# Linear attention in pairs of chunks: one score product, one output copy and one subtraction for two chunks of 128 tokens

## Chip, cores and metric

The program runs on one core of a Trainium2 chip. The metric is the device time of one execution in microseconds (us); lower is better. Engine names are those of the profile: PE is TensorE, PEld its weight loads, DVE is VectorE, ACT is ScalarE, POOL is GpSimd, SP is SyncE, which here only issues transfers.

## What is computed

Three layers follow one another. The first, which the change touches, is linear attention with a decay per head; then a gated feed-forward layer with a convolution over three tokens, then a mixture of eight experts.

```python
for t in range(S):                      # B, H, S, D = 2, 8, 768, 64
    state = gamma * state + einsum('bhd,bhe->bhde', k[:, :, t], v[:, :, t])
    y[:, :, t] = scale * einsum('bhd,bhde->bhe', q[:, :, t], state)
x = y in token order                    # (2, 768, 512)
h = relu(x @ w_in); gate = sigmoid(conv3(h)); x = (h * gate) @ w_out
out = prob[e] * (relu(x @ w1[e]) @ w2[e])   # e chosen per token
```

## The kernel before

All of the program is issued in an order written out by hand; each engine works through its own list in that order and waits on semaphores.

**Attention.** Two heads are handled together, one on the lower and one on the upper 64 partitions, so there are 8 head pairs ("heads" below). A head is cut into 6 chunks of 128 tokens, 48 chunks in all. For a chunk, `scores(c)` makes one 128 x 256 product of the keys with the two heads' queries (tile `s_ps`, L279) and multiplies it on DVE by the decays (tile `at`, L281). `output(c)` makes the chunk's addition to the state (tile `inc`, L287), which DVE adds into the state in two instructions, one per head (`st`, L292 and L294); then two products of the padded values `vz` with `at`, and one of the state before the chunk with the decayed queries, into `y` (L297 and L299). ACT copies `y` out as the upper part of a split number (L301), and DVE subtracts that copy to get the lower part (L302). That subtraction is returned as a function and is issued one chunk later. All these products are in 32-bit floats, and each shows as two records per product in the trace.

**The loop** (L424 to L447) issues `scores` of chunk i, then `output` of chunk i - 2, then the subtraction of the chunk before, then `advance()`. `advance()` moves the side work on by a step: `prepare()` of the next head (copies of the queries on ACT, the decay of queries on POOL at L253, the decay of keys on ACT, and the padded values at L274), and `convert()` for the 16 pieces of the weights `w_in` and `w_out`, which arrive as 64-bit words. A conversion fetches a piece into `raw` (L143), runs two instructions on DVE (L149, L150) and one on ACT (L151), one on POOL (L153) and the split into two parts (L171, L173). The table `STARTS` says at which chunk a conversion begins, its DVE part coming six steps later, and `LOADS` says at which chunk the loads of a head's keys, queries and values are issued. From chunk 25 on, products of the feed-forward layer (tile `h_ps`, L133 to L135) fill in between, at a rate of 0.7 slices of three products a chunk.

**Buffers.** `vz` holds the padded values of a whole head, and there is one of it. `at` has 3 buffers, `inc` one, `s_ps` and `y` two each, and each head of a lane of two has two state tiles.

Of the kernel before, what the change touches and what calls it, by code (L numbers as in the profile page):

```python
# [23 lines left out]
P = 128  # L24
# [67 lines left out]
def tile_kernel(ctx, tc, cat, cst, qT, kT, kN, vN, w_in, conv_w, w_out, wg, w1, w2, out):  # L92
# [105 lines left out]
    vz = p1.tile([P, NCH, 2, P], F32, name="vz")  # L198
    zst = [p1.tile([P, P], F32, name=f"st{i}") for i in range(4)]
# [14 lines left out]
    po.memset(vz[:, :, 0, 64:128], 0.0)  # L214
    po.memset(vz[:, :, 1, 0:64], 0.0)
    xT = {}

    class Head:


        def __init__(self, b, hp, lane):
            self.b, self.hp = b, hp
            self.g = [1.0 - 2.0 ** (-5.0 - (2 * hp + j)) for j in range(2)]
            self.qz, self.st, self.at = qz[lane], zst[2 * lane:2 * lane + 2], {}
# [15 lines left out]
        def prepare(self):  # L240
            hp = self.hp
            qd = ca[:, hp, C_QD:C_QD + CH]
            for c in self.parts:
# [10 lines left out]
                for j in range(2):  # L254
# [6 lines left out]
                    if len(self.parts) > 1:  # L261
                        self.values(c, j)
                    yield 1

            if len(self.parts) == 1:
                yield 1
                for c in (range(3), range(3, 6)):
                    for j in range(2):
                        self.values(c, j)
                    yield 3  # L270

        def values(self, c, j):
            p = slice(64 * j, 64 * j + 64)
            se.activation(out=vz[:, c.start:c.stop, j, p], in_=self.kv[:, 1, c.start:c.stop, p], func=AF.Copy)  # L274

        def scores(self, c):
            tok = slice(c * CH, (c + 1) * CH)
            ps = ps1.tile([P, 2, CH], F32, tag="s", name="s_ps")
            te.matmul(ps, self.kq[:, 0, tok], self.qz[:, :, tok], start=True, stop=True)  # L279
            self.at[c] = p1.tile([P, 2, CH], F32, tag="at", name="at", bufs=3)  # L280
            ve.tensor_tensor(out=self.at[c], in0=ps, in1=self.dm, op=ALU.mult)  # L281

        def output(self, c):
            at = self.at.pop(c)
            if c + 1 < NCH:
                inc = ps1.tile([P, P], F32, tag="i", name="inc", bufs=1)
                te.matmul(inc, self.kv[:, 0, c, :], self.kv[:, 1, c, :], start=True, stop=True)  # L287
                old, new = self.st[c % 2], self.st[(c + 1) % 2]
                for j in range(2):
                    pj = slice(64 * j, 64 * j + 64)  # L290
                    if c == 0:
                        ve.tensor_copy(out=new[pj, pj], in_=inc[pj, pj])  # L292
                    else:
                        ve.scalar_tensor_tensor(out=new[pj, pj], in0=old[pj, pj], scalar=self.g[j] ** CH, in1=inc[pj, pj], op0=ALU.mult, op1=ALU.add)  # L294
            y = ps1.tile([P, CH], F32, tag="y", name="y")
            for j in range(2):
                te.matmul(y, vz[:, c, j, :], at[:, j, :], start=(j == 0), stop=(c == 0 and j == 1))  # L297
            if c > 0:
                te.matmul(y, self.st[c % 2], self.q1[:, c, :], start=False, stop=True)  # L299
            hi, lo = (self.x[:, i, c * CH:(c + 1) * CH] for i in range(2))  # L300
            se.activation(out=hi, in_=y, func=AF.Copy)  # L301
            return lambda: ve.tensor_tensor(out=lo, in0=y, in1=hi.bitcast(F32), op=ALU.subtract)  # L302
# [92 lines left out]
    seq = [(p, c) for p in range(8) for c in range(NCH)]  # L395
# [21 lines left out]
    rest = None  # L417
    LOOK = 2
# [4 lines left out]
    slices = 0  # L423
    for i in range(len(seq) + LOOK):  # L424
        if i < len(seq):
            p, c = seq[i]
            heads[p].scores(c)
            if i == 0:
# [3 lines left out]
            if i in STARTS:  # L432
                running.append([convert(*parts.pop(0)), 1])
            if i in LOADS:
                load(LOADS[i])
# [621 lines left out]
```

## Time and profile before

| | |
|---|---|
| time, median of 3 runs | 437.85 us (436.75 to 440.81) |
| profiled execution | 436.14 us |
| its span, first to last instruction | 434.4 us |
| around the span | 1.74 us |
| mean granted TensorE clock | 0.991 of full speed |

The profiled execution lies 1.71 us under the median. Attention takes the first 90 us of the span; the feed-forward layer and the routing follow, and from about 260 us the experts. In the timelines a row that stands for several instructions of one kind gives the first start and the time to the last end. Busy times of PE include the drain of a product through the array, so that two products that follow at once overlap in the view; the distance between two starts is the cost of one.

### The profile page before, as it was taken

The page shows a single profiled execution, that of the slowest core. Times are in us where ns is not written, and L with a number is a line of the kernel's source. Part 1 is how long each engine was busy: PE and PEld are TensorE (multiplying, and loading weights), DVE is VectorE, ACT ScalarE, POOL GpSimd, SP SyncE. Part 2 cuts the span into 40 slices and gives each one's busy share as a digit, 9 for nine tenths or more (in the row PEclk, how much of TensorE's full clock was granted, in tenths as well). Part 3 has the DMA queues.
Part 4 walks back from the last instruction along what each step waited for, and adds up shares of the span by engine and source line. Part 5 has one row for each costly group of instructions (what it writes and reads, how often), then busy time and mean ns, then how long its engine had stood idle before and what let it go on. Part 6 is the DMA issues. An engine that isn't in the chain of part 4 may idle for free.

```text
span 434.4 us, 7297 instructions
## 1 busy us (share of the span) xinstructions
PE 411.6 (95%) x2412; PEld 327.6 (75%) x2412; DVE 290.0 (67%) x518; ACT 259.9 (60%) x429; POOL 91.1 (21%) x92
## 2 busy tenths in 40 slices
PE   8988999997999999999899999999999999999992
PEld 7877997896998778988678776666757667777781
DVE  3798789788766350477789157757775875867750
ACT  2787776676666212576614167756776866767660
POOL 4256664213000000000000330124033213101210
PEclk9999999998999999999999999999999999999998
DMA  7989673320000101000197898999999998984001
GB/s 238 382 298 392 245 234 86 88 83 0 2 0 2 48 28 47 25 0 2 29 382 246 318 354 286 353 395 409 386 366 313 382 364 285 352 308 150 22 27 48
DMA packets 27324, 86.59 MB, mean 199 GB/s; under 512 B 3598, under 2 KB 4622, under 8 KB 27280
## 3 DMA queue, kind: packets, MB, share of 16 engines
q1 hardware_dynamic: 25200, 79.76, 50.8%
q0 software_dynamic: 2080, 6.29, 3.8%
q8 instruction: 21, 0.34, 0.3%
q14 instruction: 23, 0.19, 0.1%
HBM read 105.18 MB, written 6.55 MB: 257 GB/s over the span
## 4 chain that ended last, share of the span: by engine, by line
PE 30%; issue 26%; DMA 18%; DVE 17%; ACT 6%; POOL 1%; SPq 1%; POOLq 0%; DVEq 0%; ACTq 0%
DMA out_dram<-yo,it 16%; DVE cc L350 4%; PE x_ps L133 4%; PE x_ps L134 3%; PE x_ps L135 3%; PE h_ps L133 3%; PE y L297 3%; PE h_ps L134 3%; PE h_ps L135 3%; PE s_ps L279 2%; DVE cc L354 2%; DVE na L149 2%; ACT cc L347 2%; PE inc L287 1%; DMA kq<-in_qT_dram 1%
## 5 line engine op out<-in xcount | busy, mean ns | idle before, releaser
L133 PE MATMUL h_ps<-xT,wih 128*128 128x384 f32 x128 | 47.1, 368 | 2.3 <-ACT wc L192 2.3
L350 DVE SCALAR_TENSOR_TENSOR cc<-h,cw,cc 128x768 f32<-128x768 f32 x32 | 35.0, 1095 | 18.0 <-ACT cc L347 18.0
L859 POOL DMA_INDIRECT out_dram<-yo,it x13 | 17.7, 1359 | 137.7 <-ACT yo L858 137.7
L723 POOL DMA_INDIRECT xg<-xs,it x13 | 17.3, 1332 | 126.8 <-DMA qc<-in_w_dram 118.9
L134 PE MATMUL h_ps<-xT,wih 128*128 128x384 f32 x128 | 43.8, 342 | 0.0
L135 PE MATMUL h_ps<-xT,wil 128*128 128x384 f32 x128 | 43.7, 341 | 0.0
L133 PE MATMUL x_ps<-woh,hg 128*128 128x512 f32 x96 | 38.6, 402 | 0.0
L134 PE MATMUL x_ps<-wol,hg 128*128 128x512 f32 x96 | 37.5, 391 | 0.0
L135 PE MATMUL x_ps<-woh,hg 128*128 128x512 f32 x96 | 37.4, 390 | 0.0
L714 DVE TENSOR_TENSOR wc<-r,wc 128x1024 fp32r<-128x1024 f32 x22 | 26.0, 1221 | 15.4 <-ACT wc L713 15.4
L714 DVE TENSOR_TENSOR ws0l<-r,ws0l 128x1024 fp32r<-128x1024 f32 x22 | 26.0, 1222 | 11.2 <-ACT ws0l L713 11.0
L714 DVE TENSOR_TENSOR ws1h<-r,ws1h 128x1024 fp32r<-128x1024 f32 x22 | 26.0, 1222 | 10.5 <-ACT ws1h L713 10.0
L297 PE MATMUL y<-at,vz 128*128 128x128 f32 x192 | 30.6, 281 | 1.2 <-DVE xT L302 0.6
L714 DVE TENSOR_TENSOR ws0h<-r,ws0h 128x1024 fp32r<-128x1024 f32 x22 | 26.0, 1222 | 7.7 <-ACT ws0h L713 7.6
L279 PE MATMUL s_ps<-qz,kq 128*128 128x256 f32 x96 | 29.1, 385 | 1.0 <-issue 1.0
L153 POOL TENSOR_TENSOR na<-na,raw 128x512 int32<-128x512 int32 (+1 forms) x17 | 21.9, 1288 | 38.2 <-DVE na L150 12.6
L713 ACT ACTIVATE ws0l<-r 128x1024 fp32r<-128x1024 f32 x22 | 22.1, 1052 | 13.1 <-PE y L135 13.1
L713 ACT ACTIVATE wc<-r 128x1024 fp32r<-128x1024 f32 x22 | 22.1, 1055 | 11.9 <-PE g L135 11.9
L133 PEld LDWEIGHTS h_ps<-xT,wih 128*128 128x128 f32 x128 | 24.6, 192 | 5.5 <-ACT wc L192 2.6
L297 PEld LDWEIGHTS y<-at,vz 128*128 128x128 f32 x192 | 25.3, 191 | 3.8 <-DVE xT L302 2.3
L281 DVE TENSOR_TENSOR at<-s_ps,ca 128x256 f32<-128x256 f32 x48 | 20.2, 421 | 11.8 <-PE s_ps L279 11.7
L713 ACT ACTIVATE ws1h<-r 128x1024 fp32r<-128x1024 f32 x22 | 22.1, 1053 | 6.5 <-PE g L135 6.2
(231 smaller groups left out, 1027.3 us busy)
## 6 DMA issues: line engine op xcount, KB each, us to landing
r<-in_w_dram SPq DMA_DIRECT2D x88, 512.0 KB
qc<-in_w_dram SPq DMA_DIRECT2D x32, 512.0 KB
qs1l<-in_w_dram SPq DMA_DIRECT2D x32, 512.0 KB
raw<-in_w_in_dram SPq DMA_DIRECT2D x8, 512.0 KB
raw<-in_w_out_dram SPq DMA_DIRECT2D x8, 512.0 KB
kq<-in_qT_dram SPq DMA_DIRECT2D x7, 384.0 KB
kq<-in_kT_dram SPq DMA_DIRECT2D x7, 384.0 KB
kv<-in_vN_dram SPq DMA_DIRECT2D x7, 384.0 KB
```

The lines of the kernel that those rows point to most:

```text
L133: te.matmul(ps, lhi, rhi, start=first, stop=False)
L134: te.matmul(ps, lhi, rlo, start=False, stop=False)
L135: te.matmul(ps, llo, rhi, start=False, stop=last)
L153: po.tensor_tensor(out=a, in0=a, in1=lo, op=ALU.add)
L279: te.matmul(ps, self.kq[:, 0, tok], self.qz[:, :, tok], start=True, stop=True)
L281: ve.tensor_tensor(out=self.at[c], in0=ps, in1=self.dm, op=ALU.mult)
L297: te.matmul(y, vz[:, c, j, :], at[:, j, :], start=(j == 0), stop=(c == 0 and j == 1))
L350: ve.scalar_tensor_tensor(out=cc, in0=h[:, i:i + S], scalar=cw[:, m, i:i + 1], in1=cc, op0=ALU.mult, op1=ALU.add)
L713: se.activation(out=w[:, 0, h, :], in_=r, func=AF.Copy)
L714: ve.tensor_tensor(out=w[:, 1, h, :], in0=r, in1=w[:, 0, h, :].bitcast(F32), op=ALU.subtract)
L723: return po.indirect_dma_start(out=xg, out_offset=None, in_=xs[0:n], in_offset=bass.IndirectOffsetOnAxis(ap=it[:, j:j + 1], axis=0), bound ...
L859: po.indirect_dma_start(out=out, out_offset=bass.IndirectOffsetOnAxis(ap=it[:, j:j + 1], axis=0), in_=yo, in_offset=None, bounds_check=NT ...
```

## The change

Attention goes on by pairs of chunks. `scores(c, u)` makes two products into the two halves of one bank of `s_ps` and one multiplication of 128 x 512 by the decays, which are repeated by a broadcast. The padded values are made there as well: two copies on ACT for the two chunks of the pair, in one of two small tiles `vz`; `prepare()` makes none any more. `output(c)` makes both additions to the state in one bank of `inc`, four state updates in a row (two for a head's last pair), and the four products of `at` with the values. The products with the state are made later, in `rest()`, after a slice of the feed-forward layer and a step of the side work; there is one copy of 128 x 256 by ACT, and one subtraction of 128 x 256, issued a pair later. Each lane has three state tiles, and `at` two buffers. The loop runs over 24 pairs and looks one pair ahead, not two chunks.

```diff
-    vz = p1.tile([P, NCH, 2, P], F32, name="vz")
-    zst = [p1.tile([P, P], F32, name=f"st{i}") for i in range(4)]
+    vz = [p1.tile([P, 2, 2, P], F32, name=f"vz{i}") for i in range(2)]
+    zst = [p1.tile([P, P], F32, name=f"st{i}") for i in range(6)]
...
-        def scores(self, c):
-            tok = slice(c * CH, (c + 1) * CH)
-            ps = ps1.tile([P, 2, CH], F32, tag="s", name="s_ps")
-            te.matmul(ps, self.kq[:, 0, tok], self.qz[:, :, tok], start=True, stop=True)
-            self.at[c] = p1.tile([P, 2, CH], F32, tag="at", name="at", bufs=3)
-            ve.tensor_tensor(out=self.at[c], in0=ps, in1=self.dm, op=ALU.mult)
+        def scores(self, c, u):
+            ps = ps1.tile([P, 2, 2, CH], F32, tag="s", name="s_ps")
+            for i in range(2):
+                tok = slice((c + i) * CH, (c + i + 1) * CH)
+                te.matmul(ps[:, i], self.kq[:, 0, tok], self.qz[:, :, tok], start=True, stop=True)
+            for j in range(2):
+                pj = slice(64 * j, 64 * j + 64)
+                se.activation(out=vz[u][:, :, j, pj], in_=self.kv[:, 1, c:c + 2, pj], func=AF.Copy)
+            at = p1.tile([P, 2, 2, CH], F32, tag="at", name="at", bufs=2)
+            ve.tensor_tensor(out=at, in0=ps, in1=self.dm.unsqueeze(1).to_broadcast([P, 2, 2, CH]), op=ALU.mult)
...
+            n = 2 if c + 2 < NCH else 1
+            for i in range(n):
+                te.matmul(inc[:, i, :], self.kv[:, 0, c + i, :], self.kv[:, 1, c + i, :], start=True, stop=True)
...
+            y = ps1.tile([P, 2, CH], F32, tag="y", name="y", bufs=2)
+            for i in range(2):
+                for j in range(2):
+                    te.matmul(y[:, i, :], v[:, i, j, :], at[:, i, j, :], start=(i == 0 and j == 0), stop=False, skip_group_check=True)
+
+            def rest():
+                for i in range(2):
+                    if c + i > 0:
+                        te.matmul(y[:, i, :], self.st[(c + i) % 3], self.q1[:, c + i, :], start=False, stop=True, skip_group_check=True)
+                hi, lo = (self.x[:, i, c * CH:(c + 2) * CH].rearrange("p (c t) -> p c t", t=CH) for i in range(2))
+                se.activation(out=hi, in_=y, func=AF.Copy)
+                return lambda: ve.tensor_tensor(out=lo, in0=y, in1=hi.bitcast(F32), op=ALU.subtract)
...
+            heads[p].scores(c, n % 2)
...
+            for i in (2 * n, 2 * n + 1):
+                if i in STARTS:
+                    running.append([convert(*parts.pop(0)), 1])
+                if i in LOADS:
+                    load(LOADS[i])
...
+        if n:
+            p, c = seq[n - 1]
             rest = heads[p].output(c)
-        if todo:
-            todo()
+        if low:
+            low()
+        fill(2 * n)
         advance()
+        if n:
+            low = rest()
+        fill(2 * n + 1)
+        advance()
```

**Where instructions move.** On SP, which issues the transfers, the start of the program: `cs`, `wgs` and `in_conv_w_dram` are small constants, `kq` and `kv` are the loads of the third head, and `raw` is the first piece of `w_in`. Before:

```order
L410 DMA cs<-in_cst_dram 128x531
L411 DMA wgs<-in_wg_dram 128x36
L143 DMA raw<-in_conv_w_dram 128x48
L143 DMA raw<-in_w_in_dram 128x1024
L230 DMA kq<-in_qT_dram 128x768
L231 DMA kq<-in_kT_dram 128x768
L233 DMA ca<-in_cat_dram 128x386
L234 DMA kv<-in_vN_dram 128x768
L235 DMA kv<-in_kN_dram 128x768
```

The same place now:

```order
L412 DMA cs<-in_cst_dram 128x531
L413 DMA wgs<-in_wg_dram 128x36
L143 DMA raw<-in_conv_w_dram 128x48
L231 DMA kq<-in_qT_dram 128x768
L232 DMA kq<-in_kT_dram 128x768
L234 DMA ca<-in_cat_dram 128x386
L235 DMA kv<-in_vN_dram 128x768
L236 DMA kv<-in_kN_dram 128x768
L143 DMA raw<-in_w_in_dram 128x1024 x3
```

The load of the third head belongs to chunk 1, which is now issued together with chunk 0 and ahead of the first step of the side work, so the first piece of `w_in` has moved behind its five transfers.

On DVE, around the first conversion (L149 and L150, which read that piece), before; the first `at` is that of chunk 6 (chunks count from 0 over all heads), the one behind the conversion that of chunk 7:

```order
L281 TENSOR_TENSOR at<-s_ps,ca 128x256
L294 SCALAR_TENSOR_TENSOR st_108<-st_107,inc 64x64 x2
L302 TENSOR_TENSOR xT<-y,xT 128x128
L149 TENSOR_SCALAR na<-raw 128x512
L150 SCALAR_TENSOR_TENSOR na<-raw,na 128x512
L281 TENSOR_TENSOR at<-s_ps,ca 128x256
L302 TENSOR_TENSOR xT<-y,xT 128x128
L281 TENSOR_TENSOR at<-s_ps,ca 128x256
L292 COPY st_110<-inc 64x64 x2
```

And now; the first `at` is that of chunks 6 and 7, the one behind the conversion that of chunks 8 and 9:

```order
L274 TENSOR_TENSOR at<-s_ps,ca 128x512
L290 SCALAR_TENSOR_TENSOR st_110<-st_109,inc 64x64 x2
L302 TENSOR_TENSOR xT<-y,xT 128x256
L149 TENSOR_SCALAR na<-raw 128x512
L150 SCALAR_TENSOR_TENSOR na<-raw,na 128x512
L274 TENSOR_TENSOR at<-s_ps,ca 128x512
L288 COPY st_112<-inc 64x64 x2
L290 SCALAR_TENSOR_TENSOR st_113<-st_112,inc 64x64 x2
L302 TENSOR_TENSOR xT<-y,xT 128x256
```

The conversion stands at the same step of the side work. The state updates behind it (`st_112` is the state after chunk 6) now feed PE within the same pair, as can be seen on PE in the second head's first pair, chunks 6 and 7:

```order
L269 MATMUL s_ps<-qz_105,kq 128x256 x2
L282 MATMUL inc<-kv 128x128 x2
L294 MATMUL y<-at,vz_107 128x128 x4
L299 MATMUL y<-kq,st_112 128x128
L269 MATMUL s_ps<-qz_105,kq 128x256 x2
L282 MATMUL inc<-kv 128x128 x2
L294 MATMUL y<-at,vz_106 128x128 x4
L299 MATMUL y<-kq,st_113 128x128
L299 MATMUL y<-kq,st_111 128x128
```

The product with `st_112` follows the `inc` it is made from by four products; before, a whole chunk lay between the two.

## Rows read from the trace of the kernel before

**Rows 1.** Timeline of PE: start us, us, engine line op out<-in xcount; chunks, a slice.
```profile
21.51 0.60 PE L279 MATMUL s_ps<-qz,kq 128*128 128x256 f32 x2
...
24.16 0.60 PE L279 MATMUL s_ps<-qz,kq 128*128 128x256 f32 x2
24.59 0.38 PE L287 MATMUL inc<-kv 128*128 128x128 f32 x2
24.81 0.61 PE L297 MATMUL y<-at,vz 128*128 128x128 f32 x4
25.26 0.39 PE L299 MATMUL y<-kq,st 128*128 128x128 f32 x2
...
44.86 0.60 PE L279 MATMUL s_ps<-qz,kq 128*128 128x256 f32 x2
...
47.51 0.42 PE L133 MATMUL h_ps<-xT,wih 128*128 128x384 f32 x1
...
48.12 0.59 PE L279 MATMUL s_ps<-qz,kq 128*128 128x256 f32 x2
```
**Rows 2.** Timeline of DVE, the same chunk and an undisturbed conversion behind it.
```profile
24.79 0.42 DVE L281 TENSOR_TENSOR at<-s_ps,ca 128x256 f32<-128x256 f32 x1 [0.20 <-PE s_ps L279]
25.13 0.46 DVE L294 SCALAR_TENSOR_TENSOR st<-st,inc 64x64 f32<-64x64 f32 x2
25.62 0.29 DVE L302 TENSOR_TENSOR xT<-y,xT 128x128 fp32r<-128x128 f32 x1
25.83 0.42 DVE L149 TENSOR_SCALAR na<-raw 128x512 int32<-128x512 int32 x1
...
26.89 0.42 DVE L281 TENSOR_TENSOR at<-s_ps,ca 128x256 f32<-128x256 f32 x1
```
**Rows 3.** Groups by line: shapes, xcount, busy us, mean ns of one, idle before.
```profile
L281 DVE TENSOR_TENSOR at<-s_ps,ca 128x256 f32<-128x256 f32 x48 | 20.2, 421 | 11.8 <-PE s_ps L279 11.7
...
L801 DVE TENSOR_TENSOR tl<-tp,th 128x512 fp32r<-128x512 f32 x22 | 14.1, 684 | 3.7 <-ACT th L800 3.7
```
**Rows 4.** Timeline, all engines, a disturbed conversion and the pause of PE behind it.
```profile
29.59 1.54 POOL L253 TENSOR_TENSOR kq<-kq,ca 128x768 f32<-128x768 f32 x1 [1.18 <-DVE st L294]
...
29.82 1.59 DVE L149 TENSOR_SCALAR na<-raw 128x512 int32<-128x512 int32 x1
...
32.06 0.42 DVE L281 TENSOR_TENSOR at<-s_ps,ca 128x256 f32<-128x256 f32 x1
...
32.98 0.46 PE L287 MATMUL inc<-kv 128*128 128x128 f32 x2 [1.56 <-DVE st L294]
```
**Rows 5.** Stretches: length, busy us (x instructions) PE, PEld, DVE, ACT, POOL; PE clock, DMA share, GB/s.
```profile
21.50:45.00 23.50, 20.57 (x145) 18.16 (x144) 21.20 (x70) 17.07 (x46) 14.86 (x12) 1.00 0.88 322
45.00:90.00 45.00, 43.36 (x298) 39.73 (x297) 36.41 (x109) 32.83 (x79) 19.91 (x15) 1.00 0.51 164
```
**Rows 6.** Timeline of SP's queue: the first piece of w_in, and the fifth transfer behind it.
```profile
10.92 0.33 SPq L143 DMA_DIRECT2D raw<-in_w_in_dram  x1
...
15.21 0.33 SPq L235 DMA_DIRECT2D kv<-in_kN_dram  x1
```
**Rows 7.** Stretches as in rows 5, the start of the program.
```profile
0.00:10.90 10.90, 8.81 (x45) 8.21 (x46) 3.66 (x9) 3.03 (x6) 5.22 (x21) 1.00 0.75 238
10.90:15.20 4.30, 3.74 (x25) 2.91 (x24) 2.90 (x12) 3.99 (x9) 1.80 (x2) 1.00 1.06 399
15.20:20.00 4.80, 4.71 (x35) 4.12 (x34) 4.14 (x15) 3.17 (x9) 0.85 (x1) 1.00 1.03 398
```
**Rows 8.** Timeline of DVE, its first conversion.
```profile
17.84 0.42 DVE L149 TENSOR_SCALAR na<-raw 128x512 int32<-128x512 int32 x1
```
**Rows 9.** Stretches as in rows 5, two pauses of PE and what follows one.
```profile
30.80:33.00 2.20, 0.64 (x5) 0.27 (x3) 2.12 (x6) 1.94 (x5) 1.43 (x3) 1.00 1.01 396
...
103.30:105.80 2.50, 0.20 (x2) 0.00 (x0) 2.50 (x4) 1.47 (x4) 0.18 (x1) 1.00 0.00 0
105.80:109.40 3.60, 3.59 (x12) 3.59 (x13) 3.29 (x5) 3.45 (x7) 1.50 (x1) 0.53 0.00 0
```

More of the change, by code (lines that the diff above doesn't have):

```diff
@@ L213, in tile_kernel @@
         po.memset(z[64:128, 0, :], 0.0)
-    po.memset(vz[:, :, 0, 64:128], 0.0)
-    po.memset(vz[:, :, 1, 0:64], 0.0)
+    for z in vz:
+        po.memset(z[:, :, 0, 64:128], 0.0)
+        po.memset(z[:, :, 1, 0:64], 0.0)
     xT = {}
@@ L260, in prepare @@
                         se.activation(out=k1, in_=k1, func=AF.Copy, scale=kd)
-                    if len(self.parts) > 1:
-                        self.values(c, j)
                     yield 1
[L265 to L274, printed above, removed]
@@ L289, in output @@
+        def output(self, c):
+            at, v = self.at.pop(c)
+            inc = ps1.tile([P, 2, P], F32, tag="i", name="inc", bufs=1)
+            n = 2 if c + 2 < NCH else 1
+            for i in range(n):
+                te.matmul(inc[:, i, :], self.kv[:, 0, c + i, :], self.kv[:, 1, c + i, :], start=True, stop=True)
+            for i in range(n):
+                old, new = self.st[(c + i) % 3], self.st[(c + i + 1) % 3]
                 for j in range(2):
                     pj = slice(64 * j, 64 * j + 64)
-                    if c == 0:
-                        ve.tensor_copy(out=new[pj, pj], in_=inc[pj, pj])
-                    else:
-                        ve.scalar_tensor_tensor(out=new[pj, pj], in0=old[pj, pj], scalar=self.g[j] ** CH, in1=inc[pj, pj], op0=ALU.mult, op1=ALU.add)
@@ L295, in output @@
[L295 to L302, printed above, removed]
+                    if c + i == 0:
+                        ve.tensor_copy(out=new[pj, pj], in_=inc[pj, i, pj])
+                    else:
+                        ve.scalar_tensor_tensor(out=new[pj, pj], in0=old[pj, pj], scalar=self.g[j] ** CH, in1=inc[pj, i, pj], op0=ALU.mult, op1=ALU.add)
@@ L304, in tile_kernel @@
+            return rest
     heads = {}
@@ L422, in tile_kernel, with fill @@
     first = stream(0, range(8))
[L423 to L428, printed above, removed]
+    def fill(i):
+        while i >= FIRST and len(taken) < (i - FIRST + 1) * RATE:
+            next(first)
+            taken.append(i)
+    taken = []
+    low = None
+    for n in range(len(seq) + 1):
+        if n < len(seq):
+            p, c = seq[n]
+            heads[p].scores(c, n % 2)
+            if n == 0:
                 keep_busy(8)
@@ L431, in tile_kernel @@
                 running.append([heads[p + 1].prepare(), 2])
[L432 to L435, printed above, removed]
-            if i == 14:
+            for i in (2 * n, 2 * n + 1):
[3 more added lines that the diff above has]
+                    load(LOADS[i])
+            if n == 7:
                 running.append([small(), 1])
-        todo = rest
-        if i >= LOOK:
-            p, c = seq[i - LOOK]
+        if n:
+            p, c = seq[n - 1]
             rest = heads[p].output(c)
-        if todo:
-            todo()
+        if low:
+            low()
+        fill(2 * n)
         advance()
-        while i >= FIRST and slices < (i - FIRST + 1) * RATE:
-            next(first)
-            slices += 1
-    rest()
-    while slices % 4:
+        if n:
+            low = rest()
+        fill(2 * n + 1)
+        advance()
+    low()
+    while len(taken) % 4:
         next(first)
-        slices += 1
+        taken.append(0)
     ps_stack.close()
```

12 lines of the change are left out of this document (3 added, 9 removed).

## Prediction

> **What bounds the kernel now.** I read the stretches first, then the timelines of PE and DVE inside attention, then the groups by line for durations, then SP's queue at the start. From 21.5 to 45 us PE is busy 20.57 of 23.50 us and DVE 21.20; from 45 to 90 us PE is busy 43.36 of 45.00 and DVE 36.41 [rows 5]. PE is the engine that work is waiting on, and in the first stretch DVE is nearly as full and stops it. One chunk on PE, start to start, is 0.43 for the scores, 0.22 for `inc`, 0.45 for the two products into `y`, and 0.22 for the product with the state, which has the shape of `inc` [rows 1]: 1.32 us. A head has six of these, less one state product and one `inc`: 7.48 us.
>
> Between the scores at 21.51 and those at 44.86 lie 15 chunks [rows 1], 23.35 us. Their work is 15 x 7.48 / 6 = 18.7, so PE lost 4.65 us there. Where it went: a conversion occupies DVE for 1.06 us when nothing disturbs it, from 25.83 to 26.89 [rows 2]. It took 2.24 us, from 29.82 to 32.06, when POOL was multiplying (29.59 to 31.13); PE then stood still until the state update came, at 32.98 [rows 4]. From 45 to 90 us PE is idle 1.64 us [rows 5]. The view counts the drain of a product as busy (0.60 busy against a pitch of 0.43, rows 1), so each stop is 0.17 longer than shown; with some nine stops that is about 3.2 us lost.
>
> **What the change does to PE's own work: nothing.** The products keep their number and shapes: 0.86 + 0.43 + 0.90 + 0.43 = 2.64 us a full pair, 2.42 for a head's first and last pair. What can change is only where PE waits. I take the parts in order of time.
>
> **1. The start.** The loads of the third head now go ahead of the first piece of `w_in`. On SP that piece takes the fifth place behind its old one, where the issue was at 15.21, against 10.92 [rows 6]. Sizes follow from the shapes: a head's four loads and its constants 1.77 MB, `cs` 0.27, the piece 0.52. Ahead of and with the piece stood two heads, 4.4 MB; now three, 6.1 MB. By 10.9 us 2.6 MB had moved, by 15.2 us 4.3, by 20.0 us 6.2, the last two at 398 to 399 GB/s [rows 7]: by bytes the piece arrives at about 19.8. In time from issue: it was used at 17.84 without a wait [rows 8], so it needs at most 6.9 us, and arrives by 22.1 at the latest. I take the middle, 21.0.
>
> DVE and ACT both stand on it, and each works in order. Behind L149 on DVE are `at` of chunks 8 and 9 and the state after chunk 6, which PE needs for its next product. So: 21.0 + 1.06 (conversion) + 0.60 (`at` of 128 x 512) + 0.46 (two copies of the state) + 0.12 (DVE to PE: 32.06 + 0.34 + 0.46 against 32.98, rows 2 and 4) = 23.24, and with 0.22 for the product 23.46. Before, the same state of the work (outputs to chunk 7, scores to 9) was reached at 21.51 [rows 1]. Cost: 2.0 us, between 0.7 and 3.1 by the two ends for the arrival. The 0.60 is the mean of a 128 x 512 operation on data in PSUM, 684 ns, against 421 for 128 x 256 [rows 3], added to the pitch of 0.34 of the small one [rows 2].
>
> **2. The clock.** PE, which would reach that product at about 20 to 21 us, stands for 2.3 to 3.5 us. A pause of 2.5 us (103.3 to 105.8) was followed by 3.60 us at a granted clock of 0.53, 1.2 GHz in place of 2.4; one inside 30.8 to 33.0 left it at 1.00 [rows 9]. The nearest row is the longer pause: 3.60 x 0.47 = 1.7 us lost. Bounds are 0 and twice that, 3.4, if it happens again.
>
> The Trainium skill, "TensorE: Matmul & The Clock Gate", section "HAM oscillation — how this bites in real kernels", says that a wait on a transfer which leaves the array idle long enough puts it back to half its clock. By that rule this wait costs twice, once as a wait and once afterwards, and the 1.7 us stand; by the shorter pause of the trace they would be nothing. The trace bears the rule out at 103.3 us.
>
> **3. Pairs from there to 45 us.** DVE per full pair before: 2 x (0.34 + 0.49 + 0.21) = 2.08 us, from the starts at 24.79, 25.13, 25.62 and 25.83 [rows 2]. Now: 0.60 + 0.92 for four updates + 0.34 for a subtraction of 128 x 256 (the pitch of `at` at that size) = 1.86. That is 0.22 a pair freed, and 0.78 of DVE's time free in a pair of 2.64. Against that, the second state product now waits for an update of its own pair. Scores done at 0.43 + 0.63 (24.16 to 24.79) = 1.06 after the pair's start, `at` to 1.66, two updates to 2.12, plus 0.12: 2.24, against PE's own 2.42. In a head's first and last pair PE is there at 2.20: 0.04 to 0.1 lost. So an undisturbed conversion is 0.28 late and costs 0.28 - 0.18, about 0.1, and a disturbed one 2.24 - 0.78 - 0.18 = 1.3. Before there were four in this stretch, two of them disturbed; I keep that: 2.6 + 0.2, 0.2 for the small one of `conv_w`, and 0.4 for first and last pairs: 3.4 in place of 4.65, a gain of 1.25. Ends: 4.65 saved if POOL falls elsewhere, 1.8 lost if all four are disturbed (5.2 + 0.6 = 5.8, and a little more for late pairs).
>
> **4. Pairs from 45 to 90 us.** A slice of three products, 0.61 us (47.51 to 48.12, rows 1), comes 1.4 times a pair, mostly between the updates and the products that need them. DVE is then free for 0.78 + 0.85 = 1.6 us a pair, more than a conversion. I keep 1.1 us (a wait for ACT's copy and one disturbed conversion) of the 3.2: gain 2.1, between 0 and 3.2.
>
> **5. ACT and POOL.** POOL's work is the same. ACT makes 24 copies out of `y` for 48, and 48 small ones of the values for 32; it is busy 17.07 of 23.50 us [rows 5], and the values are needed a pair after they are made. I count nothing; behind the first piece ACT is late too, but `at` and the state end the wait later. Without that cover, 0.5 us a pair of late values would be exposed.
>
> **6. Behind 90 us.** The order stays, so a shift goes through. The pause at 103.3 [rows 9] I leave as it is: DVE is busy in all of it, with the same instructions; its bounds are 0 and 4.2 (2.5 + 1.7) saved.
>
> **Sum** on the profiled execution, 436.14 us: + 2.0 + 1.7 - 1.25 - 2.1 = + 0.35, so 436.5. The median lies 1.71 higher: 437.85 + 0.35 = 438.2 us.
>
> **Rivals.**
> - *The clock holds* through the wait at the start. For it: the pause inside 30.8 to 33.0. Against: that was shorter. 438.2 - 1.7 = 436.5.
> - *The piece of `w_in` is there in time*, since the 16 engines need not serve transfers in order of issue. Against: the DMA share is 1.03 to 1.06 [rows 7], so nothing is free to overtake with. Then step 1 gives back the 0.56 + 0.09 us that PE is idle from 10.9 to 20 us [rows 7] with their drains, 1.0 in all: 437.85 - 1.0 - 1.25 - 2.1 = 433.5.
> - *The pause at 103.3 closes*, as DVE comes less late out of attention: 438.2 - 4.2 = 434.0. Against: the chain there hangs on DVE alone.
> - *Slower: state updates within the pair.* PE now waits for an update of the same pair, and each conversion that POOL disturbs lands there for 1.3 us. Twelve conversions follow the first one inside attention. With six disturbed and 0.1 for each of the rest: 7.8 + 0.6 + 0.7 kept for ACT = 9.1 lost against 7.85 before, and with 3.7 from the start 437.85 + 1.25 + 3.7 = 442.8. It decides from six of twelve on. For it: two of four were disturbed. Against: slices lie in between from 45 us on.
>
> **How the numbers follow.** Forecast 0.45, own range 435.5 to 441; clock holds 0.18; piece in time 0.13; pause closes 0.08; slower 0.16. About 1%, 4.4 us, is what a measurement of this kernel can tell from no change. Faster by more, under 433.5: half of the piece in time, half of the closed pause, some of the two likeliest cases: 0.23. Slower by more, over 442.2: most of the slower rival and the forecast's tail: 0.19. Within 1%: 0.58. The range, 432.5 to 442.8, reaches from below the piece in time to the slower rival.
>
> **What would show it.** Right: L149 at its first start waits for a transfer of `raw` until about 21 us, a state product of PE then waits for DVE until about 23, and the clock falls below 1.00 between 20 and 30 us; DVE's `at` at 0.68 us; PE idle from 45 to 90 us under 1 us. Wrong: no wait at 17 to 23 us, or stops of 1 us and more behind most conversions. If attention ends before 86 us, the start was cheap; if after 93, the pairs wait for each other.

## The result, and the profile after

The changed kernel takes 442.53 us (median of 4 runs, 442.06 to 444.64) against 437.3 us for the kernel before beside it (4 runs, 435.43 to 440.81): ratio 1.0108, 95% interval 1.0065 to 1.0152. It is 1.1% slower. The forecast was 438.2 us and no change within 1%; the time lies at the upper end of the range. The profiled execution took 442.06 us with a span of 440.2 us, against 436.14 and 434.4 before.

The start first. SP's queue, DVE's timeline and PE's timeline of the changed kernel, in this order:

```profile
13.81 0.33 SPq L236 DMA_DIRECT2D kv<-in_kN_dram  x1
14.63 9.55 SPq L143 DMA_DIRECT2D raw<-in_w_in_dram  x3
```
```profile
16.08 0.43 DVE L302 TENSOR_TENSOR xT<-y,xT 128x256 fp32r<-128x256 f32 x1
21.25 0.43 DVE L149 TENSOR_SCALAR na<-raw 128x512 int32<-128x512 int32 x1 [4.75 <-DMA raw<-in_w_in_dram]
21.71 0.69 DVE L150 SCALAR_TENSOR_TENSOR na<-raw,na 128x512 int32<-128x512 int32 x1
22.32 0.68 DVE L274 TENSOR_TENSOR at<-s_ps,ca 128x512 f32<-128x512 f32 x1
22.93 0.46 DVE L288 COPY st<-inc 64x64 f32<-64x64 f32 x2
```
```profile
17.74 1.06 PE L294 MATMUL y<-at,vz 128*128 128x128 f32 x8
23.49 0.69 PE L299 MATMUL y<-kq,st 128*128 128x128 f32 x2 [4.70 <-issue]
23.97 1.91 PE L269 MATMUL s_ps<-qz,kq 128*128 128x256 f32 x4
...
38.42 0.49 PE L299 MATMUL y<-kq,st 128*128 128x128 f32 x2 [2.69 <-DVE st L290]
...
46.84 1.03 PE L269 MATMUL s_ps<-qz,kq 128*128 128x256 f32 x4
```

The first piece of `w_in` is issued at 14.63 where it was 10.92 [rows 6], and DVE waits 4.75 us for it where its first conversion found it there at 17.84 [rows 8]. Behind that conversion stand the `at` and the state copies that PE needs, so PE stands still for 4.70 us. The releaser "issue" at 23.49 means that the view names none; DVE's list above does. The scores of chunk 10, which started at 21.51 before [rows 1], start at 23.97. The four records in that row (two products) span 1.91 us, for 1.03 at 46.84: PE runs at about half its clock.

```profile
20.00:22.50 2.50, 0.00 (x0) 0.00 (x0) 1.21 (x3) 1.25 (x3) 0.00 (x0) 1.00 0.34 138
22.50:25.00 2.50, 1.51 (x5) 1.36 (x6) 1.72 (x6) 2.42 (x6) 2.03 (x2) 0.72 0.14 21
25.00:27.50 2.50, 2.50 (x14) 2.32 (x13) 1.34 (x4) 1.66 (x5) 2.35 (x2) 0.60 0.90 304
...
45.00:90.00 45.00, 43.26 (x306) 40.90 (x304) 37.93 (x90) 31.99 (x76) 22.76 (x17) 1.00 0.56 186
```

These are stretches of the changed kernel with the columns of [rows 5]. The granted clock (third from the end) was 1.00 until PE had stood still; then it was 0.72 and 0.60.

The pause of 2.69 us at 38.42 is the other thing that was not there in this size. DVE and POOL around it:

```profile
31.67 0.69 DVE L274 TENSOR_TENSOR at<-s_ps,ca 128x512 f32<-128x512 f32 x1
...
34.08 1.92 DVE L150 SCALAR_TENSOR_TENSOR na<-raw,na 128x512 int32<-128x512 int32 x1
35.91 0.17 DVE L149 TENSOR_SCALAR na<-raw 128x24 int32<-128x24 int32 x1
36.11 1.27 DVE L150 SCALAR_TENSOR_TENSOR na<-raw,na 128x24 int32<-128x24 int32 x1
37.31 0.68 DVE L274 TENSOR_TENSOR at<-s_ps,ca 128x512 f32<-128x512 f32 x1
37.91 0.96 DVE L290 SCALAR_TENSOR_TENSOR st<-st,inc 64x64 f32<-64x64 f32 x4
```
```profile
31.88 1.29 POOL L153 TENSOR_TENSOR na<-na,raw 128x512 int32<-128x512 int32 x1 [4.37 <-ACT xT L301]
33.84 1.61 POOL L254 TENSOR_TENSOR kq<-kq,ca 128x768 f32<-128x768 f32 x1 [0.67 <-ACT qz L251]
36.07 1.28 POOL L153 TENSOR_TENSOR na<-na,raw 128x512 int32<-128x512 int32 x1 [0.63 <-DVE na L149]
```

L150 takes 0.69 us when nothing disturbs it (21.71 above). At 34.08 POOL is in an instruction that ends at 33.84 + 1.61 = 35.45, and L150 ends 0.55 us later. The one of 128 x 24 at 36.11 ends at 37.38, POOL's at 37.35. Both stood until POOL was done, one behind the other in the same pair, because `small()`, the conversion of `conv_w`, falls on that pair too. The `at` at 31.67, which reads PSUM, runs beside POOL's instruction of 31.88 and takes its usual 0.69.

Where the 5.8 us between the two profiled spans arise:

| place (start, us) | before | after | difference |
|---|---|---|---|
| scores of chunk 10 | 21.51 | 23.97 | +2.46 |
| scores of chunk 24 | 42.19 | 46.84 | +4.65 |
| scores of chunk 26 | 46.49 | 50.57 | +4.08 |
| last state product of attention | 89.6 | 92.4 | +2.8 |
| first product into `x_ps` | 136.0 | 138.4 | +2.4 |
| last instruction ends | 434.4 | 440.2 | +5.8 |

The lines behind the rows of chunks 24 and 26, before and then after (that of chunk 24 after stands above). Between the two lies the second of before's pauses behind a disturbed conversion:

```profile
42.19 0.60 PE L279 MATMUL s_ps<-qz,kq 128*128 128x256 f32 x2
43.85 0.46 PE L287 MATMUL inc<-kv 128*128 128x128 f32 x2 [1.07 <-DVE st L294]
...
46.49 0.59 PE L279 MATMUL s_ps<-qz,kq 128*128 128x256 f32 x2
```
```profile
50.57 1.02 PE L269 MATMUL s_ps<-qz,kq 128*128 128x256 f32 x4
```

The lines behind the fourth and fifth row, by tile (xcount: ns min/median/max, first to last start), before and then after:

```profile
L299 PE MATMUL y<-kq,st x80: 275/275/275, 12.2 to 89.6; 128*128 128x128 f32 x80
L133 PE MATMUL x_ps<-woh,hg x96: 388/389/505, 136.0 to 245.5; 128*128 128x512 f32 x96
```
```profile
L299 PE MATMUL y<-kq,st x80: 272/275/471, 10.7 to 92.4; 128*128 128x128 f32 x80
L133 PE MATMUL x_ps<-woh,hg x96: 389/392/505, 138.4 to 247.9; 128*128 128x512 f32 x96
```

Attention and what follows up to 138 us explain +2.4. From there on the program is the same in both kernels, and still 3.4 us more appear; what they are is a question for the runs.

### The profile page after: what moved, and what is told of

Same layout as the page of the kernel before. It is cut to its first block, busy times and chain, and to the rows that moved or that the text cites. A ratio compares the mean times of both kernels' runs of the same rounds, so it can differ in the third digit from the quotient of the medians.

```text
span 440.2 us, 7246 instructions
## 1 busy us (share of the span) xinstructions
PE 412.7 (94%) x2412; PEld 329.7 (75%) x2412; DVE 289.0 (66%) x470; ACT 258.3 (59%) x421; POOL 92.0 (21%) x96
## 4 chain that ended last, share of the span: by engine, by line
PE 34%; issue 26%; DVE 17%; DMA 17%; ACT 4%; POOL 1%; POOLq 0%; DVEq 0%
DMA out_dram<-yo,it 16%; DVE cc L352 4%; PE s_ps L269 4%; PE x_ps L133 4%; PE x_ps L134 3%; PE x_ps L135 3%; PE h_ps L133 3%; PE y L294 3%; PE h_ps L134 3%; PE h_ps L135 3%; DVE cc L356 2%; DVE na L150 2%; PE y L299 2%; ACT cc L349 2%; PE inc L282 1%
## 5 line engine op out<-in xcount | busy, mean ns | idle before, releaser
L133 PE MATMUL h_ps<-xT,wih 128*128 128x384 f32 x128 | 46.6, 364 | 0.9 <-ACT wc L192 0.7
L134 PE MATMUL h_ps<-xT,wih 128*128 128x384 f32 x128 | 43.3, 338 | 0.0
L134 PE MATMUL x_ps<-wol,hg 128*128 128x512 f32 x96 | 37.5, 391 | 0.0
L269 PE MATMUL s_ps<-qz,kq 128*128 128x256 f32 x96 | 26.3, 399 | 0.0
L375 ACT ACTIVATE h<-h_ps 128x384 f32<-128x384 f32 x32 | 15.6, 486 | 17.2 <-PE h_ps L135 14.6
L294 PE MATMUL y<-at,vz 128*128 128x128 f32 x192 | 25.6, 277 | 0.0
L495 ACT ACTIVATE xn<-x_ps 128x512 f32<-128x512 f32 x10 | 6.0, 600 | 33.0 <-PE x_ps L135 15.7
```

Source lines behind the costliest of these rows:

```text
L133: te.matmul(ps, lhi, rhi, start=first, stop=False)
L134: te.matmul(ps, lhi, rlo, start=False, stop=False)
L269: te.matmul(ps[:, i], self.kq[:, 0, tok], self.qz[:, :, tok], start=True, stop=True)
L294: te.matmul(y[:, i, :], v[:, i, j, :], at[:, i, j, :], start=(i == 0 and j == 0), stop=False, skip_group_check=True)
L375: se.activation(out=pads[m % 3][:, 1 + u * HF:1 + (u + 1) * HF], in_=ps[:, 0:HF], func=AF.Relu)
```

## The experiments

My theory: the loads of the third head, now ahead of the first piece of `w_in`, cost the wait and the fall of the clock behind it, and the pairs themselves gain. The rival: the pairs are slower, because a state product waits for an update of its own pair. A table at the end of this section puts all runs side by side.

**The order of the loads, alone and undone.** In the changed kernel, the loads that belong to an odd chunk (1, 11 and 15: the third, fourth and fifth head) are issued behind the state products of the pair:

```diff
-                if i in LOADS:
+                if i in LOADS and i % 2 == 0:
                     load(LOADS[i])
...
         fill(2 * n)
         advance()
+        if 2 * n + 1 in LOADS:
+            load(LOADS[2 * n + 1])
```

> The changed kernel, but the loads that belong to an odd chunk are issued behind the state products of the pair, so that the first piece of w_in stands ahead of the third head's loads again. Nothing of the computation changes. Theory (the start costs 2.0 to 2.5 us and the clock that falls after it 1.7): no wait for that piece near 17 to 23 us, granted clock 1.00 from 20 to 30 us, the last state product of the attention 4 to 5 us earlier than in the changed kernel (87 to 88 against 92.3), about 438 us in all, and 435 if the 3.4 us that came on in the experts' stage hang on the shift. Rival (the state updates within the pair are what costs): the wait goes, but the pairs lose it again behind state waits, and the time stays at 441 or more.

Measured: 436.89 us against 438.32, ratio 0.9965 (0.9931 to 1.0000), so hardly to be told from the kernel before. PE's timeline, and its stretch at 20 us:

```profile
19.56 1.03 PE L269 MATMUL s_ps<-qz,kq 128*128 128x256 f32 x4
...
32.55 0.49 PE L299 MATMUL y<-kq,st 128*128 128x128 f32 x2 [2.70 <-DVE st L290]
...
40.98 1.03 PE L269 MATMUL s_ps<-qz,kq 128*128 128x256 f32 x4
...
44.70 1.02 PE L269 MATMUL s_ps<-qz,kq 128*128 128x256 f32 x4
```
```profile
20.00:25.00 5.00, 5.00 (x39) 4.81 (x38) 3.68 (x12) 3.51 (x11) 2.92 (x2) 1.00 0.98 347
```

The wait is gone and the clock stays up; chunk 10 is reached at 19.56, 4.41 us ahead of the changed kernel, and attention ends at 86.5 in place of 92.4. The rival would have kept the time at 441 or more. The pause of 2.70 us is still there. The other half of the test puts the new order of the loads into the kernel before, chunk by chunk:

```diff
-    LOADS = {1: 2, 11: 3, 15: 4, 20: 5, 28: 6, 32: 7}
+    LOADS = {0: 2, 11: 3, 15: 4, 20: 5, 28: 6, 32: 7}
```

> The kernel before, chunk by chunk, with one number of the table of loads changed: the third head's loads are issued one chunk earlier, hence ahead of the first piece of w_in, as in the changed kernel. Nothing of the computation changes. Theory (the order of the loads alone makes the wait): VectorE and ScalarE wait for that piece to about 21 us, the state product behind it comes 2 to 3 us later than before, the granted clock falls under 0.9 between 20 and 30 us, and the time is 2 to 4 us above the kernel before (439 to 441). Rival (it hurts only the pairs, since chunk by chunk the scores run further ahead): the conversion waits as long but TensorE has work, and the time is that of the kernel before within 1 us.

Measured: 442.92 us against 438.32, ratio 1.0103 (1.0071 to 1.0135). DVE's timeline, and two stretches:

```profile
20.93 0.43 DVE L149 TENSOR_SCALAR na<-raw 128x512 int32<-128x512 int32 x1 [3.17 <-DMA raw<-in_w_in_dram]
```
```profile
20.00:25.00 5.00, 2.23 (x14) 2.21 (x15) 3.64 (x12) 2.68 (x5) 1.57 (x2) 0.91 0.31 88
25.00:30.00 5.00, 5.00 (x30) 4.71 (x29) 2.72 (x11) 2.97 (x8) 2.79 (x2) 0.74 0.96 361
```

One number in a table, without any pairs, makes the kernel before as slow as the change made it. The loss, 4.6 us, is above the 2 to 4 that I had written; the end of attention moved by 4.7 (94.3 against 89.6). Of these, 3.5 us stand at chunk 10 (25.04 against 21.51), behind the wait, and 1.2 more come on by chunk 24 (46.94 against 42.19), where the clock was low; behind that nothing is added.

**State updates first.** The run with the late loads, and DVE multiplies the scores behind the pair's state updates (`decays` is that multiplication, which `scores` now hands back as a function):

```diff
-            heads[p].scores(c, n % 2)
+            decays = heads[p].scores(c, n % 2)
...
             rest = heads[p].output(c)
+        if n < len(seq):
+            decays()
```

> The run with the late odd loads, with one more edit: VectorE multiplies the pair's scores by the decays behind the state updates of the pair instead of ahead of them. Nothing of the computation changes. Theory (the second state product of a pair waits for the first's update, and a conversion disturbed by GpSimd ahead of it makes that a pause): the update comes 0.7 us sooner in each pair, the pauses behind state updates (2.7, 0.5, 0.6 us in the changed kernel) shrink, and the time is 1 to 3 us under the run with the late odd loads. Rival (the state is not what TensorE waits for, or the masked scores are then late instead): the same time within 1 us, with waits for the masked scores in place of those for the state.

Measured: 433.45 us against 438.32, ratio 0.9891 (0.9848 to 0.9934), and 3.4 us under the run with the late loads alone, where 1 to 3 was expected. The pauses of 0.28, 0.50, 0.58, 0.33 and 0.22 us behind state updates went, but for one of 0.48; attention ends at 84.6, which is 1.9 us earlier. The expectation that the longest shrinks was wrong: it is 2.68 us.

**The conversion of conv_w elsewhere.** The same edit in three kernels, here in the run with the state updates first (in the kernel before, chunk 4 in place of 14):

```diff
-            if n == 7:
+            if n == 2:
                 running.append([small(), 1])
```

> The run with the state updates first, with the conversion of the 24 columns of conv_w issued at the third pair instead of the eighth, away from GpSimd's long multiplications. Nothing of the computation changes. Theory (a VectorE instruction with both operands in SBUF stands until the GpSimd instruction that runs is over; the two of 128x24 took 1.52 and 1.21 us for that and made the pause of 2.68 us at 32.1): the two take about 0.2 us each, the pause at 32 us falls under 1 us, the attention ends 1.5 to 2.7 us earlier (82 to 83 against 84.6), the whole takes 431 to 432 us against 433.5. Rivals: another conversion meets GpSimd's work instead and the pause moves (the attention's end within 0.5 us of 84.6); or the columns have not landed at 15 us and VectorE waits there (slower).

Measured: 433.48 us against 438.33, ratio 0.9892 (0.9843 to 0.9942): no gain in time. DVE's timeline, POOL's and PE's:

```profile
15.21 0.18 DVE L149 TENSOR_SCALAR na<-raw 128x24 int32<-128x24 int32 x1 [0.15 <-DMA raw<-in_conv_w_dram]
15.43 0.18 DVE L150 SCALAR_TENSOR_TENSOR na<-raw,na 128x24 int32<-128x24 int32 x1
...
20.15 1.33 DVE L318 CAST identr<-cs 128x128 fp32r<-128x128 f32 x1
...
28.51 1.59 DVE L149 TENSOR_SCALAR na<-raw 128x512 int32<-128x512 int32 x1
```
```profile
19.59 1.81 POOL L254 TENSOR_TENSOR kq<-kq,ca 128x768 f32<-128x768 f32 x1
...
28.28 1.54 POOL L254 TENSOR_TENSOR kq<-kq,ca 128x768 f32<-128x768 f32 x1 [0.66 <-ACT qz L251]
```
```profile
31.27 0.49 PE L303 MATMUL y<-kq,st 128*128 128x128 f32 x2 [1.18 <-DVE st L294]
```

The two small instructions take 0.18 us away from POOL, as expected. But now the large conversion at 28.51 stands until POOL's L254 ends at 29.82, and a copy at 20.15 until 21.40. The pause fell to 1.18 us and attention ends at 83.7, 0.9 earlier: theory and rival each had half.

> The changed kernel with that one edit alone (conv_w's conversion at the third pair). Nothing of the computation changes. Theory: the wait for the first piece of w_in and the clock's fall stay, the pause of 2.69 us at 38.4 goes under 1 us, the attention ends 1.5 to 2.5 us earlier than in the changed kernel (90 to 91 against 92.4), the whole takes 440.5 us against 442.5. Rival (the pause moves to another conversion): within 0.5 us of the changed kernel.

In the changed kernel the edit gave 441.71 us against 438.33, ratio 1.0076 (1.0042 to 1.0109), with a pause of 1.29 us at 38.1, not under 1; attention ends at 91.9, only 0.5 us earlier than 92.4, as the rival says. The time is 1.8 us under the unedited kernel's beside it (443.50, below).

> The kernel before with the conversion of conv_w's columns issued at chunk 4 instead of 14. Nothing of the computation changes. Theory: the wait of 1.56 us at 33.0 shrinks, the attention ends 0.5 to 1.5 us earlier than in the kernel before, the whole 437 us against 438.3. Rival (chunk by chunk the scores run two chunks ahead, and the wait at 33 comes from the conversion of 512 columns): the same time within 0.5 us.

In the kernel before it gave 439.43 us against 438.33, ratio 1.0036 (1.0004 to 1.0069); the wait at 33 us is 1.56 as before, so there it is the conversion of 512 columns [rows 4], as the rival says. The time is 1.1 us above, not within the rival's 0.5; in the profile attention ended 0.4 earlier (89.2).

**The clock alone.** PE is kept busy through the wait in the changed kernel with products that nobody reads (tile `lg`):

```diff
+    BUSY = 22
...
         if n:
+            if n == 4:
+                keep_busy(BUSY)
             low = rest()
```

> The changed kernel with 22 products of 128x128 on TensorE, whose result nobody reads, in the place where it waits for the first piece of w_in (17.7 to 23.5 us): some 4.8 us of work that fits into the wait. Nothing that the kernel returns changes. Theory (the clock falls because TensorE was idle, and costs 1.7 us): the state product still starts near 23.5 us, the granted clock stays at 1.00 from 20 to 30 us, and the attention ends 1.7 us earlier than in the changed kernel, as does the whole (440.8 against 442.5). Rival (the fall of the clock comes from something else, or costs nothing since VectorE sets the pace there): the clock or the end of the attention stays within 0.5 us of the changed kernel's.

Measured: 443.80 us against 438.32, ratio 1.0123 (1.0068 to 1.0178), attention ends at 92.5: no gain. DVE's state copies, and PE:

```profile
23.07 0.47 DVE L288 COPY st<-inc 64x64 f32<-64x64 f32 x2
```
```profile
19.29 5.08 PE L208 MATMUL lg<-st 128*128 128x128 f32 x44
24.21 0.39 PE L299 MATMUL y<-kq,st 128*128 128x128 f32 x2
```

The products ran on beyond the wait: in the changed kernel the state product follows the start of the copies by 0.56 us (22.93 and 23.49), which would be 23.6 here, and it came at 24.21, when they were through. The clock stayed at 1.00 from 20 to 30 us, and the pause at 38.42 came at 37.41; but behind that pause it fell now (0.62 and 0.69 in the stretches from 37.5 to 42.5), which it had not in the changed kernel, and the 1.0 us was given back. To take that pause out of the test, the same products (20 of them) went into the changed kernel with the early conversion of conv_w, which ran once more beside it:

> The run of the changed kernel with the early conversion of conv_w, plus 20 products of 128x128 on TensorE, whose result nobody reads, in the wait for the first piece of w_in. Nothing that the kernel returns changes. Here the second long pause (2.69 us) is down to 1.29 us, so that a clock kept up at 20 to 30 us has no such pause behind it to fall in. Theory (the clock's fall behind the wait costs 1.7 to 3.5 us, 3.4 in that run's profile at 0.72 and 0.60): clock 1.00 from 20 to 45 us, the attention ends 2 to 3.5 us earlier than 91.9 (88.5 to 90), the whole 439 to 440 us against 441.7. Rival (what the clock gives is lost again behind VectorE's state updates or later): the clock stays up, and the attention ends within 1 us of 91.9 and the whole within 1 us of 441.7.

> The changed kernel with the early conversion of conv_w once more, unedited, beside the run with the 20 products on one chip. Expected: 441 to 442 us, a wait near 4 us that ends at 23.5 to 24, and a granted clock under 0.9 from 20 to 30 us.

Measured, both against 437.77 us: 440.14 with the products, ratio 1.0030 (0.9996 to 1.0065), 440.99 without, ratio 1.0072 (1.0030 to 1.0115). Stretches without the products, then with them:

```profile
25.00:30.00 5.00, 5.00 (x25) 4.56 (x25) 4.02 (x9) 3.13 (x10) 3.08 (x2) 0.66 0.69 267
```
```profile
25.00:30.00 5.00, 5.00 (x39) 4.78 (x38) 3.85 (x14) 4.12 (x11) 3.12 (x2) 1.00 0.73 269
```

The wait ends at 24.4 and 24.6 in the two, and attention at 91.9 and 90.2. So in these two profiles the fall of the clock costs 1.7 us of attention, under the 2 to 3.5 that I had expected and over the rival's 1: I had counted the low clock of the wait as well, and while PE stands still that costs nothing. The whole moved by 0.85 us, inside the intervals, so how much of the 1.7 comes through is not shown.

**Repeats.** Three kernels once more, for second profiles:

> The changed kernel once more, unedited, for its time beside the others on one chip and for a second profile. Theory (its attention ends 2.6 us later than before's and the other 3 us of the profiled run are scatter of the gather of tokens ahead of the experts and of the experts' stage): the attention ends within 0.5 us of 92.4 again, the wait of TensorE for the gathered rows (1.39 us in the first profile, 0.55 in before's) comes out anywhere between 0.5 and 3 us, and the median is 2.5 to 4.5 us above before's. Rival (the later attention makes the experts' stage longer): both the gather's wait and the length from the first product of the experts to the end (175.5 us) come out as they did, and the median is 5 us above before's.

> The run with the late odd loads once more, unedited, for a second profile: its first one lay 3.6 us under the median of its 12 runs. Expected if the pause of 2.7 us near 32.5 is followed by a low clock in some executions, as in the second profile of the changed kernel: a granted clock under 0.9 somewhere from 32 to 45 us, and the attention ends later than 86.5 by what that costs, 1 to 3.5 us. Expected if the scatter lies behind the attention: the attention ends within 0.5 us of 86.5, and the stretch from the first product of the routing's input to the end is over 300 us (298.8 in the first profile).

> The run with the state updates first once more, unedited, beside the run with the late odd loads on one chip. Expected: 432.5 to 435 us, 1 to 3.5 us under the other, the attention ends at 84 to 85 us, and the pause near 32 us is 2.7 us again.

The changed kernel: 443.50 us against 438.33, ratio 1.0123 (1.0073 to 1.0172). Its attention ended at 95.9, not within 0.5 us of 92.4. By the pause of 2.69 us it was 1.1 us behind the first profile (39.49 against 38.42), as the wait ended 0.6 us later and the low clock behind it lasted longer. The other 2.5 us came behind the pause, which was as long as in the first profile and was now followed by half the clock.

```profile
39.49 0.80 PE L299 MATMUL y<-kq,st 128*128 128x128 f32 x2 [2.69 <-DVE st L290]
```
```profile
37.50:40.00 2.50, 0.51 (x2) 0.51 (x3) 2.38 (x7) 0.00 (x0) 2.32 (x3) 0.76 1.02 393
40.00:42.50 2.50, 2.50 (x10) 2.14 (x9) 0.86 (x2) 1.96 (x6) 0.86 (x2) 0.50 1.01 381
42.50:45.00 2.50, 2.50 (x13) 2.50 (x13) 2.23 (x8) 0.00 (x0) 0.73 (x2) 0.50 1.02 385
```

In the first profile the clock was 1.00 in all three. From the first product into `g` with the experts' weights `ws1h` to the end it took 175.3 us, as the rival said (175.5 in the first), and the median is 5.2 us above before's, as it said too, where the theory had 2.5 to 4.5. But that length is 175.7 with the earliest attention of all (ending at 83.7) and 172.4 where attention ended at 90.2, so it does not go with the shift. The late loads: 435.86 us against 437.67, ratio 0.9947 (0.9914 to 0.9980); the state updates first: 433.55, ratio 0.9919 (0.9891 to 0.9946). Behind the pause near 32 us the clock fell in both second profiles (to 0.84 and 0.66 from 30 to 35 us) and in neither first one; attention ended 1.1 and 2.9 us later than in the first, at 87.6 and at 87.4, where I had expected 84 to 85 for the latter. Of the two guesses on the scatter the first held, and the second in its half on the stretch behind: 301.3 us for the late loads, where it had been 298.8.

| kernel | median, us | beside it: before | attention ends | first `x_ps` to the end |
|---|---|---|---|---|
| before | | | 89.6 | 298.4 |
| changed | 442.53; 443.50 | 437.30; 438.33 | 92.4; 95.9 | 301.8; 302.1 |
| late odd loads | 436.89; 435.86 | 438.32; 437.67 | 86.5; 87.6 | 298.8; 301.3 |
| before, early load | 442.92 | 438.32 | 94.3 | 301.9 |
| late loads, state first | 433.45; 433.55 | 438.32; 437.67 | 84.6; 87.4 | 300.9; 302.0 |
| the same, conv_w early | 433.48 | 438.33 | 83.7 | 303.2 |
| changed, conv_w early | 441.71; 440.99 | 438.33; 437.77 | 91.9; 91.9 | 300.8; 301.8 |
| before, conv_w early | 439.43 | 438.33 | 89.2 | 300.5 |
| changed, PE kept busy | 443.80 | 438.32 | 92.5 | 302.8 |
| changed, conv_w early, PE kept busy | 440.14 | 437.77 | 90.2 | 302.7 |

The last column is code that no kernel here touches. It varies from 298.4 to 303.2 us over 14 profiles, and the profile of before has the lowest value. Part of that is PE's wait for the first gathered rows of the experts; before, and with conv_w early and PE kept busy:

```profile
246.94 1.13 PE L809 MATMUL tp<-cs,xg 128*128 128x128 f32 x8 [0.55 <-DMA xg<-xs,it]
```
```profile
250.16 2.05 PE L822 MATMUL tp<-cs,xg 128*128 128x128 f32 x8 [3.55 <-DMA xg<-xs,it]
```

The 3.4 us that the two first profiles differ by behind 138 us lie within this scatter, with before's at the quick end: that execution, 436.14 us, also lies 1.2 to 2.2 us under before's medians.

## Why the prediction was right or wrong

**Step 1, the start: right.** The piece was taken to arrive at 21.0 and was used at 21.25; the state product was put at 23.24 and came at 23.49; the cost of 2.0 us was 2.46 at chunk 10, of which 0.25 is the later arrival and 0.26 the state product at half the clock (from 23.49 to 23.97, 0.48 in place of 0.22). Against the run that only puts the loads back it is 4.41 us: the pairs were 1.95 ahead by then (19.56 against 21.51), and the wait ate that and 2.46 more. What I had not thought through is that the price hangs on this order and not on the pairs: the kernel before pays it too.

**Step 2, the clock: right for the fall it names, too few of them.** The 1.7 us measured 1.7 with PE kept busy, and 1.45 in the first profile (22.87 us from chunk 10 to 24, less 21.42 in the run with the late loads). Missing is the second pause: 2.69 us at 38.42 is another place where the clock falls in some executions and not in others. From that pause to the end of attention the fall cost 2.5 us in the second profile and 1.1 with PE kept busy. I had weighed one wait against the two pauses of [rows 9], one with a fall behind it and one without, and never asked it of the pauses in the pairs.

**Step 3, pairs to 45 us: wrong, and this is the step that failed.** I had -1.25 us; the run with the late loads, where no clock is in the way, took 25.14 us from chunk 10 to 26 (44.70 - 19.56) against 24.98 before (46.49 - 21.51): +0.16, so 1.4 us are missing. (To chunk 24 it is 21.42 against 20.68, but before's second disturbed conversion, which the step counts, makes its pause of 1.07 us between chunks 24 and 25.) The term that was mis-sized is "0.2 for the small one of `conv_w`": it took 0.17 + 1.27 = 1.44 us of DVE, beside POOL. And I had let POOL disturb conversions at 1.3 us each in different pairs; a disturbed one cost 1.92 - 0.69 = 1.23, as put, but it shared a pair with the small one, and by my own working a pair has 0.78 us of DVE's time free. I had also seen only L149 disturbed [rows 4], not L150. The bound "1.8 lost" does not follow from its terms: 5.8 - 4.65 is 1.15, and the "little more" has no number.

**Step 4, pairs from 45 to 90 us: right in kind, too large.** From chunk 26 to the last state product the lag went from 4.08 to 2.8 us and, with the late loads, the lead from 1.8 to 3.1: 1.3 us gained in both, in place of 2.1. The "some nine stops" behind the 3.2 us are six in the trace of the kernel before, which makes it 2.7; and of the stops that were left, four in the changed kernel stand before a state product (0.50, 0.58, 0.33 and 0.22 us), which the 1.1 that I kept did not count. PE's idle time from 45 to 90 us, 45.00 - 43.26 = 1.74, is not under 1 us as I said it would be, and no less than the 1.64 of [rows 5]; but 306 records ran in that busy time, where it was 298. The gain is in what the busy time hides, stops shorter than the drain. From chunk 10 to 16, where PE is idle for 0.09 us before and not at all with the late loads, it can be seen alone: 7.99 us (21.51 to 29.50) against 7.71 (19.56 to 27.27).

**Step 5: right.** No wait of PE in the changed kernel's attention names ACT's copies or the padded values. **Step 6, behind 90 us: right in kind.** +2.8 at the end of attention is +2.4 at the first `x_ps`.

**The sum.** +2.46 + 1.45 + 0.16 - 1.3 - 0.4 = +2.4 us for the first profile, against +0.35: of the 2.05 too little, 1.4 is step 3, 0.8 step 4 and 0.5 the start, and the clock and the way to `x_ps` gave some back. The medians moved by 5.2 in both comparisons. The first profile is a mild execution: its mean granted clock, 0.984, is the second highest of the changed kernel's ten, of which eight have 0.973 to 0.981 (the kernel before beside the later six has a median of 0.990). By that measure most executions lost more to the clock than that profile shows, as the second profile did (0.973), whose first `x_ps` came 7.0 us after before's. How often the clock falls behind the second pause is not shown by 2 profiles, and the split of the rest stays open.

**The rivals.** "State updates within the pair" gave 442.8, the nearest number, for another reason: its pauses are there, but with the loads put back the same pairs are faster than before. Its pauses are a real cost all the same: with the updates ahead of the multiplication the medians are 3.4 and 2.3 us lower, though attention ended only 1.9 and 0.2 us earlier in the profiles. That rival sets the upper end of the range, so that the time lies inside it is luck in part. "The piece in time" is what the late loads made of it; they measured 436.89 and 435.86, not 433.5. In their first profile attention ended 3.1 us before that of the kernel before, in place of the 4.35 that this rival adds up: the start gave 1.95 where it has 1.0, steps 3 and 4 gave 2.2 less. In the second profile the clock fell behind the pause and took 1.1 of that. The clock did not hold. The pause at 103.3 became two, of 0.95 and 0.74 us, in the first profile, and 0.95 and 1.86 in the second. The sign "after 93, the pairs wait for each other" came up in the second profile, at 95.9, for the clock and not for that.

With the loads put back and the state updates first, the pairs beat both kernels: 433.45 and 433.55 us, 0.8 to 1.1% under before.

## What to carry to other kernels

When a loop is made coarser, look up in every table that is keyed by its steps what now goes first: here two steps that became one moved five transfers ahead of the one that an in-order engine needed next, and that alone cost the kernel before 4.6 us. Price side work on an engine by the other engine whose instructions it may have to wait for, and count how many such pieces can land in one step, not how many there are in all. A pause is charged twice when the clock falls behind it, and not in every execution, so one profile does not tell its price.

## What the runs showed of the hardware

In attention a VectorE instruction whose operands all lie in SBUF that starts while a GpSimd `TENSOR_TENSOR` runs ended only after that, in all 14 profiles: 0.18 became 1.27 us (128 x 24) and 0.69 became 1.92 (128 x 512); the 128 x 128 copy from `cs` took 1.33, where it takes 0.22 in the run with the state updates first. Instructions of VectorE with an operand in PSUM (`at`, 0.69 beside POOL) take their usual time. What GpSimd runs matters: VectorE's subtraction `ws1h<-r,ws1h` in the experts, all in SBUF, takes 1.22 us alone and when it starts inside a GpSimd gather (`DMA_INDIRECT`) or `MEMSET`. The waits for `TENSOR_TENSOR` agree with the Trainium skill, "SBUF — State Buffer", section "Who interferes with whom", which has VectorE's second pair of ports shared with GpSimd, held by one of them for a whole instruction, and needed by instructions with two inputs in SBUF (L150) or in a two-port mode (L149 and the copy can be that: 128 x 512 in 0.42 us where L150 takes 0.69).

A pause of TensorE of about 2.69 us was followed by half the clock in four of seven profiles that had it ahead of 45 us (the changed kernel's second, PE kept busy with the conversion late, and the second ones of the late loads and of the state updates first), and by a clock of 1.00 in the other three, with the same instructions on either side in the two profiles of a kernel. The waits of 3.9 to 4.9 us at the start were followed by a low clock in each of the four profiles of the changed kernel with and without the early conversion, and so was the one of 3.36 us in the kernel before with the early load. What a fall behind the pause of 2.69 us cost, from there to the end of attention, was 1.1, 1.1, 2.5 and 2.7 us against a profile with the same instructions and no fall there.
